# Attention feeding a Mish MLP on one core: three tiled stays per four heads instead of four, shared two-bank PSUM tiles, and Mish in half blocks

## The chip, the cores and the metric

The kernel runs on one core of one Trainium2 chip. The metric is the device time of one execution in microseconds (us), as the median of several executions. A *span* is the time from the first to the last instruction of the profiled execution; it is about 1.7 to 3 us shorter than the device time.

## The reference

Eight batches, twelve heads, 448 tokens, head size 64. The attention's softmax has an extra 1 in its denominator, its output is laid side by side over the heads, and an MLP with Mish follows.

```python
scores = scale * np.matmul(q, k.transpose(0, 1, 3, 2))        # q, k, v: (8, 12, 448, 64)
m = np.max(scores, axis=-1, keepdims=True)
e = np.exp(scores - m)
attn = e / (np.sum(e, axis=-1, keepdims=True) + np.exp(-m) + 1e-09)
x = np.matmul(attn, v)                                         # then heads side by side: (3584, 768)
h = x @ w_in                                                   # w_in: (768, 2048)
g = h * np.tanh(softplus(h))                                   # Mish
out = g @ w_out                                                # w_out: (2048, 768)
```

Multiplying numerator and denominator by exp(m) gives exp(s) / (1 + sum exp(s)), which is what the kernel computes.

## The kernel before

The program goes through the batches in passes. In pass p, TensorE does the attention of batch p between the first MLP product of batch p-1 (the `h` units, six matmuls of 448 columns) and the second one of batch p-2 (the `o` units, eight matmuls of 384 columns). A *group* is four heads, that is two pairs of heads; a pass has three groups, and groups are numbered from 0 over all batches.

Three kinds of matmul use TensorE in different shapes ("tiling modes"): the `h` and `o` units fill the array (128 x 128). The scores put two heads into two row halves (64 x 128). The sums and the product with v put four heads into four column strips (128 x 32). An uninterrupted run of tiled matmuls between full-size work is called a *stay* here.

```python
s_pool = ...tile_pool(name="s_ps", bufs=2, space=PSUM)     # score tiles, two banks each
x_pool = ...tile_pool(name="x_ps", bufs=2, space=PSUM)     # av tiles, one bank each
m_pool = ...tile_pool(name="m_ps", bufs=2, space=PSUM)     # everything else, one bank each

def sums(g):                                   # denominators of four heads
    den = m_pool.tile([128, 512], FP32, tag="m", name="den_ps")
    side_by_side(den, g, lambda c, t: ones[0:P, :])                     # 16 tiled matmuls
    rc = work.tile([128, S], FP32, tag="rc", name="rc")
    nc.scalar.activation(out=rc, in_=den[:, 0:S], func=AF.Ln, bias=1.0)
    nc.scalar.activation(out=rc, in_=rc, func=AF.Exp, scale=-1.0)       # rc = 1 / (1 + den)
    rc_t[g] = rc

def attend(g, s):                              # half s of the head size
    ...
    av = x_pool.tile([128, 512], FP32, tag="x", name="av_ps")           # a tile for each half
    side_by_side(av, g, lambda c, t: ...v_t[g]...[:, c, t, s])          # 16 tiled matmuls
    nc.vector.tensor_mul(x_t[b][:, gi, s, :], av[:, 0:S], rc_t[g])

def mish(b):                                   # the whole batch at once, on ScalarE
    ...
    nc.scalar.activation(out=gt[:, :, o : o + TAIL], in_=h_sb[:, :, MAIN:S], func=AF.Mish)
    for i in range(4):
        ...
        nc.scalar.activation(out=gm[:, f, :], in_=h_sb[:, f, 0:MAIN], func=AF.Mish)
    nc.scalar.preload_act_table_set("natural_log_exp_and_others")

def slot(j, units, pre=0, mish_of=None):       # one pair of heads; j even also does a group's av
    ...
    run(units, pre)
    g = j // 2 - 1 if j % 2 == 0 and j >= 2 else None
    if g is not None:
        sums(g)
    ...
    scores(j, (0, 1))                          # four matmuls, two exps on ScalarE
    if g is not None:
        attend(g, 0)
        attend(g, 1)
    run(units, (len(units) + 1) // 2)
    ...
    scores(j, (2, 3))
    run(units)
```

`side_by_side` issues 16 matmuls into four column strips; `scores(j, tiles)` issues two matmuls for each score tile and one exp that reads it. A score tile's buffer is free again when its exp has read it.

The softmax here doesn't subtract the row's maximum and nothing guards it: scores larger than these inputs give would overflow.

## Time and profile before

| | |
|---|---|
| device time, median | 459.04 us (3 runs, 457.97 to 459.19) |
| span | 456.1 us |
| TensorE busy | 435.1 us, 95% |
| a pass from 150 us on, mean of four | 51.45 us |
| granted TensorE clock, mean | 0.98 |

Three lines of the page of the profile: the busy time of each engine, the granted TensorE clock in tenths over 40 slices of the span, and the engines of the chain of work that ended last.

```profile
PE 435.1 (95%) x3424; PEld 211.2 (46%) x3424; DVE 139.5 (31%) x232; ACT 265.1 (58%) x323; POOL 87.9 (19%) x144
...
PEclk9898999799989999999999999999999999999999
...
PE 84%; ACT 7%; DMA 6%; POOL 1%; issue 1%; DVE 0%; POOLq 0%
```

TensorE (PE) is the bound. Only a change of its own instruction stream, or of what it waits for, can move the time.

The timeline of PE over one group of a later pass follows: start and length in us, line, output and inputs, number of matmuls. The difference of two starts is what a block costs, because consecutive matmuls overlap at their ends.

```profile
201.61 0.94 PE L177 MATMUL den_ps<-e,ones 112*32 112x448 bf16 x16
202.48 0.59 PE L154 MATMUL s_ps<-qk 64*112 64x448 bf16 x4
202.99 1.70 PE L177 MATMUL av_ps<-e,v_b 112*32 112x448 bf16 x32
204.62 2.44 PE L211 MATMUL h_ps<-xT,w_in_sb 128*128 128x448 bf16 x12
207.00 0.59 PE L154 MATMUL s_ps<-qk 64*112 64x448 bf16 x4
207.52 2.44 PE L211 MATMUL h_ps<-xT,w_in_sb 128*128 128x448 bf16 x12
...
215.67 0.94 PE L177 MATMUL den_ps<-e,ones 112*32 112x448 bf16 x16
```

Nothing waits here: no line carries a bracket with idle time. The stay den, scores, av takes 3.01 us (201.61 to 204.62), and three stays of four score matmuls follow in the group.

What waits there are stand early in the run. These lines of the list of waits give the total in us, how often, and the longest.

```profile
PE s_ps L154 <- ACT e L161: 7.9, 7, 4.4
...
PE tr_ps L137 <- DMA kq<-in_k_dram: 2.9, 2, 2.2
```

The 7.9 us are mostly the first two Mish blocks, which keep ScalarE away from the exps that free the score tiles.

### The profile page before, as it was taken

What the parts mean: (1) busy time and instruction counts of PE and PEld (TensorE: products, weight loads), DVE (VectorE), ACT (ScalarE), POOL (GpSimd) and SP (SyncE); (2) the same over time, 40 slices, a digit from 0 to 9 for tenths busy, and PEclk for the clock granted to TensorE, in tenths of its full rate; (3) what the DMA queues carried; (4) which work ended last, traced back from release to release, by engine and by line L of the source; (5) the groups of instructions that cost most, each with busy time, mean ns of one, the idle gap of its engine ahead of it and who ended that gap; (6) DMA issues with size and microseconds to landing.
All of it is one profiled execution on the core that took longest, in us unless ns stands there. A gap on an engine that the chain in (4) does not pass through costs nothing.

```text
span 456.1 us, 8023 instructions
## 1 busy us (share of the span) xinstructions
PE 435.1 (95%) x3424; PEld 211.2 (46%) x3424; DVE 139.5 (31%) x232; ACT 265.1 (58%) x323; POOL 87.9 (19%) x144
## 2 busy tenths in 40 slices
PE   8789998599979999999999999999999999999995
PEld 3334443244534446444554446444554445555563
DVE  2223543133203442244313442234313442210121
ACT  5586559754865558564865558564775559442200
POOL 6444214011111420142011410143011100000000
PEclk9898999799989999999999999999999999999999
DMA  9999999241357911893156911794056401210122
GB/s 203 202 204 204 189 165 220 62 101 44 84 132 163 225 59 36 166 295 94 30 140 163 239 55 34 182 273 101 22 144 163 95 1 34 71 36 27 44 69 69
DMA packets 77540, 55.21 MB, mean 121 GB/s; under 512 B 36544, under 2 KB 73920, under 8 KB 77504
## 3 DMA queue, kind: packets, MB, share of 16 engines
q1 hardware_dynamic: 64288, 44.51, 41.2%
q0 software_dynamic: 13216, 10.19, 14.5%
q8 instruction: 26, 0.43, 0.4%
q14 instruction: 10, 0.08, 0.1%
HBM read 45.61 MB, written 11.01 MB: 124 GB/s over the span
## 4 chain that ended last, share of the span: by engine, by line
PE 84%; ACT 7%; DMA 6%; POOL 1%; issue 1%; DVE 0%; POOLq 0%
PE h_ps L211 31%; PE o_ps L263 31%; PE s_ps L154 9%; PE av_ps L177 8%; PE den_ps L177 4%; ACT e L161 3%; DMA kq<-in_q_dram 3%; DMA w_in_sb<-in_moe_w_in_dram 3%; ACT gm L240 2%; POOL kq L100 1%; PE tr_ps L137 1%; ACT L241 1%; ACT L237 1%; ACT gt L237 0%; POOL w_in_sb L293 0%
## 5 line engine op out<-in xcount | busy, mean ns | idle before, releaser
L161 ACT ACTIVATE e<-s_ps 112x896 bf16<-112x896 f32 x192 | 164.5, 912 | 103.5 <-PE s_ps L154 103.3
L211 PE MATMUL h_ps<-xT,w_in_sb 128*128 128x448 bf16 x768 | 159.5, 356 | 1.1 <-DVE h_sb L219 1.1
L263 PE MATMUL o_ps<-w_out_sb,gm 128*128 128x384 bf16 x768 | 132.1, 328 | 0.0
L211 PEld LDWEIGHTS <-w_in_sb 128*128 128x128 bf16 x768 | 70.6, 98 | 81.1 <-issue 23.5
L263 PEld LDWEIGHTS <-gm 128*128 128x128 bf16 x768 | 74.1, 98 | 55.3 <-issue 7.8
L219 DVE COPY h_sb<-h_ps 128x448 f32<-128x448 f32 x112 | 69.9, 624 | 96.6 <-PE h_ps L211 94.4
L271 DVE COPY o_sb<-o_ps 128x384 f32<-128x384 f32 x56 | 31.2, 558 | 140.7 <-PE o_ps L263 135.4
L154 PE MATMUL s_ps<-qk 64*112 64x448 bf16 x384 | 61.3, 382 | 8.9 <-ACT e L161 7.9
L116 POOL CAST kq<-k_f 112x512 bf16<-112x512 f32 x36 | 22.1, 614 | 192.6 <-DMA k_f<-in_k_dram 173.0
L203 DVE TENSOR_TENSOR xT<-av_ps,rc 128x448 bf16<-128x448 f32 x48 | 29.9, 625 | 48.9 <-PE av_ps L177 46.0
L177 PE MATMUL av_ps<-e,v_b 112*32 112x448 bf16 x768 | 41.2, 357 | 0.0
L154 PEld LDWEIGHTS <-qk 64*112 64x112 bf16 x384 | 19.6, 126 | 46.2 <-issue 42.3
L240 ACT ACTIVATE gm<-h_sb 128x1536 bf16<-128x1536 f32 x28 | 39.1, 1467 | 0.0
L189 ACT ACTIVATE rc<-den_ps 128x448 f32<-128x448 f32 x24 | 13.1, 546 | 39.2 <-PE den_ps L177 39.2
L120 POOL CAST v_b<-v_f 112x512 bf16<-112x512 f32 x36 | 22.1, 613 | 49.5 <-PE av_ps L177 38.6
L177 PEld LDWEIGHTS <-v_b 112*32 112x32 bf16 x768 | 18.6, 97 | 19.9 <-issue 6.7
L177 PE MATMUL den_ps<-e,ones 112*32 112x448 bf16 x384 | 23.6, 367 | 0.0
L116 POOL CAST kq<-q_f 112x512 bf16<-112x512 f32 x36 | 22.1, 614 | 5.2 <-DMA q_f<-in_q_dram 4.1
L263 PE MATMUL o_ps<-w_out_sb,gt 128*128 128x384 bf16 x128 | 22.5, 326 | 0.0
L223 ACT ACTIVATE gm<-h_ps 128x384 bf16<-128x384 f32 x16 | 7.8, 490 | 21.2 <-PE h_ps L211 21.2
L263 PEld LDWEIGHTS <-gt 128*128 128x128 bf16 x128 | 12.0, 98 | 9.5 <-issue 2.0
L177 PEld LDWEIGHTS <-ones 112*32 112x32 bf16 x384 | 8.4, 97 | 12.9 <-issue 9.3
(27 smaller groups left out, 102.9 us busy)
## 6 DMA issues: line engine op xcount, KB each, us to landing
k_f<-in_k_dram SPq DMA_DIRECT2D x37, 224.0 KB, 3.6
q_f<-in_q_dram SPq DMA_DIRECT2D x37, 224.0 KB, 3.8
v_f<-in_v_dram SPq DMA_DIRECT2D x36, 224.0 KB, 4.0
w_in_sb<-in_moe_w_in_dram POOLq DMA_DIRECT2D x8, 384.0 KB, 12.6
w_out_sb<-in_moe_w_out_dram POOLq DMA_DIRECT2D x4, 768.0 KB, 17.4
out_dram<-o_sb SPq DMA_DIRECT2D x8, 336.0 KB, 2.9
out_dram<-o_sb SPq DMA_DIRECT2D x8, 288.0 KB, 2.7
out_dram<-o_sb SPq DMA_DIRECT2D x8, 240.0 KB, 2.7
```

Source lines behind the costliest of these rows:

```text
L116: nc.gpsimd.tensor_copy(out=mb[:, i].rearrange("p t h d -> p h t d"), in_=loaded.pop((j, name)).rearrange("p h (t d) -> p h t d", d=D),)
L120: nc.gpsimd.tensor_copy(out=vb[:, o : o + 2], in_=loaded.pop((j, "v")))
L154: nc.tensor.matmul(sp[0:P, h, 0:S], lhsT=qk[r, 0, t * P : (t + 1) * P], rhs=qk[r, 1, :], start=True, stop=True,)
L161: nc.scalar.activation(out=e_t[j][:, t], in_=sp[0:P, :, 0:S], func=AF.Exp, scale=SCALE)
L177: nc.tensor.matmul(ps[c * 32 : c * 32 + 32, 0:S], lhsT=weights(c, t), rhs=e_t[2 * g + c // 2][:, t, c % 2, :], start=(t == 0), stop=(t == ...
L189: nc.scalar.activation(out=rc, in_=den[:, 0:S], func=AF.Ln, bias=1.0)
L203: nc.vector.tensor_mul(x_t[b][:, gi, s, :], av[:, 0:S], rc_t[g])
L211: nc.tensor.matmul(hp[:, 0:S], lhsT=w_in_sb[:, dm // 2, dm % 2, ff * 128 : (ff + 1) * 128], rhs=x_t[b][:, dm // 2, dm % 2, :], start=(dm = ...
L219: nc.vector.tensor_copy(out=h_sb[:, ff, :], in_=hp[:, 0:S])
L240: nc.scalar.activation(out=gm[:, f, :], in_=h_sb[:, f, 0:MAIN], func=AF.Mish)
L263: nc.tensor.matmul(op[:, 0:HALF], lhsT=lhs, rhs=w_out_sb[:, ff, n * HALF : (n + 1) * HALF], start=(ff == 0), stop=(ff == FF_T - 1),)
L271: nc.vector.tensor_copy(out=o_sb[:, n * HALF : (n + 1) * HALF], in_=op[:, 0:HALF])
```

## The change

The intent: fewer changes of the tiling mode on TensorE, fewer gaps around Mish, earlier arrival of k and q at the start, a shorter tail. Two pairs of heads become one `group_slot` with three stays: den, av and two score tiles; three score tiles; three score tiles. For three score tiles in one stay, three two-bank PSUM tiles are needed. The separate av tiles had to go, so av takes one of the three, with its two halves in its two banks. Mish runs in two halves, one in each of two groups (`gates_of` says which half a `group_slot` runs).

```diff
-    s_pool = ctx.enter_context(tc.tile_pool(name="s_ps", bufs=2, space=PSUM))
-    x_pool = ctx.enter_context(tc.tile_pool(name="x_ps", bufs=2, space=PSUM))
+    s_pool = ctx.enter_context(tc.tile_pool(name="s_ps", bufs=3, space=PSUM))
...
-    def attend(g, s):
+    def attend(g):
...
-        av = x_pool.tile([128, 512], FP32, tag="x", name="av_ps")
-        side_by_side(av, g, ...)
-        nc.vector.tensor_mul(x_t[b][:, gi, s, :], av[:, 0:S], rc_t[g])
+        av = s_pool.tile([128, 2, 512], FP32, tag="s", name="av_ps")
...
+        for s in range(2):
+            side_by_side(av[:, s], g, lambda c, t: vs[:, c, t, s])
+            nc.vector.tensor_mul(x_t[b][:, gi, s, :], av[:, s, 0:S], rc)
...
-    def mish(b):
+    def mish(b, i):                  # half i: 8 of the 16 blocks of h
...
+    def group_slot(u, after_a, after_b, after_c, gates_of=None):
+        prepare(2 * u)
+        sums(u - 1)
+        if gates_of is not None:
+            mish(*gates_of)
+        attend(u - 1)
+        if 2 * u < J:
+            scores(2 * u, (0, 1))
+        run(after_a)
...
+        scores(2 * u, (2, 3))
+        scores(2 * u + 1, (0,))
+        run(after_b)
...
+        scores(2 * u + 1, (1, 2, 3))
+        run(after_c)
...
+            else:                    # passes 3 to 7
+                n = len(m2)
+                group_slot(u, cut(m2, n // 2 - 4), cut(m1, 4), cut(m1, 4))
+                group_slot(u + 1, cut(m1, 5), m1, cut(m2, 2), (p - 1, 0))
+                group_slot(u + 2, cut(m2, 4), cut(m2, n // 4 - 1 & ~1), m2, (p - 1, 1))
```

Cut: the order of the loads (k and q of groups 2 and 3 go ahead of most of w_in), the units of passes 1 and 2, and the tail, where the last eviction is split over VectorE and ScalarE and its two stores go out from two queues.

More of the change, by code (lines that the diff above doesn't have):

```diff
@@ L191, in sums @@
         rc_t[g] = rc
-    def attend(g, s):
+    def attend(g):
         b, gi = divmod(g, GRP)
-        if gi == 0 and s == 0:
+        if gi == 0:
             x_t[b] = work.tile([128, GRP, 2, S], BF16, tag="xT", name="xT")
-        av = x_pool.tile([128, 512], FP32, tag="x", name="av_ps")
-        side_by_side(
-            av,
-            g,
-            lambda c, t: v_t[g].rearrange("p c (t d s) -> p c t s d", s=2, d=D // 2)[:, c, t, s],
-        )
-        nc.vector.tensor_mul(x_t[b][:, gi, s, :], av[:, 0:S], rc_t[g])
-        if s == 1:
-            e_t.pop(2 * g), e_t.pop(2 * g + 1), v_t.pop(g)
-            rc_t.pop(g)
+        av = s_pool.tile([128, 2, 512], FP32, tag="s", name="av_ps")
+        vs = v_t.pop(g).rearrange("p c (t d s) -> p c t s d", s=2, d=D // 2)
+        rc = rc_t.pop(g)
+        for s in range(2):
+            side_by_side(av[:, s], g, lambda c, t: vs[:, c, t, s])
+            nc.vector.tensor_mul(x_t[b][:, gi, s, :], av[:, s, 0:S], rc)
+        e_t.pop(2 * g), e_t.pop(2 * g + 1)
     def mm1(b, ff, direct):
@@ L236, in mish @@
         n = FF_T // 4
-        nc.scalar.activation(out=gt[:, :, o : o + TAIL], in_=h_sb[:, :, MAIN:S], func=AF.Mish)
-        for i in range(4):
-            f = slice(i * n, (i + 1) * n)
+        f = slice(2 * i * n, (2 * i + 2) * n)
+        nc.scalar.activation(out=gt[:, f, o : o + TAIL], in_=h_sb[:, f, MAIN:S], func=AF.Mish)
+        for f0 in (2 * i * n, (2 * i + 1) * n):
+            f = slice(f0, f0 + n)
             nc.scalar.activation(out=gm[:, f, :], in_=h_sb[:, f, 0:MAIN], func=AF.Mish)
@@ L270, in mm2 @@
         if part == 1:
-            nc.vector.tensor_copy(out=o_sb[:, n * HALF : (n + 1) * HALF], in_=op[:, 0:HALF])
+            cols = slice(n * HALF, (n + 1) * HALF)
+            if b == B - 1 and t == NC:
+                q0, q1 = n * HALF, n * HALF + HALF // 2
+                nc.vector.tensor_copy(out=o_sb[:, q0:q1], in_=op[:, 0 : HALF // 2])
+                nc.scalar.copy(o_sb[:, q1 : q1 + HALF // 2], op[:, HALF // 2 : HALF])
+                for i, eng in enumerate((nc.sync, nc.scalar)):
+                    rows = out[(b - 1 + i) * S : (b + i) * S, cols]
+                    rows = rows.rearrange("(p t) n -> t p n", t=NT)[NT - 1, P - TAIL : P]
+                    eng.dma_start(out=rows, in_=o_sb[i * TAIL : (i + 1) * TAIL, cols])
+                return
+            nc.vector.tensor_copy(out=o_sb[:, cols], in_=op[:, 0:HALF])
             if n == 1:
@@ L303, in load_w_out @@
         )
-    fetch = {
-        2: [lambda: load_cast(3, "kq"), lambda: load_w_in(3)],
-        3: [lambda: load_cast(3, "v"), lambda: load_w_out(0)],
-        4: [lambda: load_cast(4, "kq")],
-        5: [lambda: load_cast(4, "v"), lambda: load_w_out(1)],
-        6: [lambda: load_cast(5, "kq")],
-        7: [lambda: load_cast(5, "v"), lambda: load_w_out(2), lambda: load_w_out(3)],
-    }
     def first_slot(j):
-        for f in fetch.get(j, ()):
-            f()
         g = j // 2 - 1 if j % 2 == 0 and j >= 2 else None
+        if j % 2:
+            g3 = 3 + j // 2
+            load_cast(g3, "kq")
+            if j == 1:
+                load_cast(2, "v")
+            else:
+                load_cast(g3 - 1, "v")
+            load_w_in(1 + j // 2)
         scores(j, (0,))
@@ L330, in first_slot @@
         if g is not None:
-            attend(g, 0)
-            attend(g, 1)
+            attend(g)
         scores(j, (3,))
@@ L339, in run, with prepare @@
             units.pop(0)()
-    def slot(j, units, pre=0, mish_of=None):
-        for f in fetch.get(j, ()):
-            f()
+    def prepare(j):
         if SW <= j + 2 < J:
@@ L349, in slot @@
             load(j + 4)
-        run(units, pre)
-        g = j // 2 - 1 if j % 2 == 0 and j >= 2 else None
-        if g is not None:
-            sums(g)
-        if mish_of is not None:
-            mish(mish_of)
-        if j < J:
-            scores(j, (0, 1))
-        if g is not None:
-            attend(g, 0)
-            attend(g, 1)
-        run(units, (len(units) + 1) // 2)
-        if j + 1 < J:
-            transposes(j + 1)
-        if j < J:
-            scores(j, (2, 3))
-        run(units)
+    def group_slot(u, after_a, after_b, after_c, gates_of=None):
[7 more added lines that the diff above has]
+        run(after_a)
+        if 2 * u >= J:
+            return
+        if u == GRP:
+            transposes(2 * u + 1)
+        transposes(2 * u + 2)
+        prepare(2 * u + 1)
+        scores(2 * u, (2, 3))
+        scores(2 * u + 1, (0,))
+        run(after_b)
+        transposes(2 * u + 3)
+        scores(2 * u + 1, (1, 2, 3))
+        run(after_c)
     def cut(m, n):
@@ L379 @@
         load_cast(1, "kq")
+        load_cast(2, "kq")
         load_w_in(0)
         load_cast(1, "v")
-        load_cast(2, "kqv")
-        load_w_in(1)
-        load_w_in(2)
         idle(8)
@@ L388 @@
         transposes(0)
-        for p in range(B):
-            m1 = mm1_units(p - 1) if p >= 1 else []
+        for j in range(NPAIR):
+            first_slot(j)
+        for p in range(1, B):
+            m1 = mm1_units(p - 1)
             m2 = mm2_units(p - 2) if p >= 2 else []
-            for i in range(NPAIR):
-                j = p * NPAIR + i
-                if p == 0:
-                    first_slot(j)
-                elif p == 1:
-                    slot(j, cut(m1, (2, 3, 3, 3, 3, 2)[i]))
-                elif p == 2:
-                    if i == 0:
-                        slot(j, cut(m1, 6), mish_of=0)
-                    elif i in (1, 3):
-                        slot(j, cut(m1, 1) + cut(m2, 2) + cut(m1, 1), pre=1)
-                    elif i < 5:
-                        slot(j, cut(m1, 4), pre=1)
-                    else:
-                        slot(j, m2, pre=1)
-                elif i == 0:
-                    slot(j, cut(m2, len(m2) - 10 + p % 2 * -2), pre=1)
-                elif i < 5:
-                    slot(j, cut(m1, 4), pre=1)
-                else:
-                    slot(j, m2, pre=1)
-                if i == 4 and p >= 2:
-                    mish(p - 1)
-                    run(cut(m2, len(m2) * 2 // 3))
+            u = p * GRP
+            if p == 1:
+                load_w_out(0)
+                group_slot(u, cut(m1, 1), cut(m1, 2), cut(m1, 2))
+                load_cast(5, "v")
+                load_w_out(1)
+                load_w_out(2)
+                load_w_out(3)
+                group_slot(u + 1, cut(m1, 2), cut(m1, 2), cut(m1, 2))
+                group_slot(u + 2, cut(m1, 2), cut(m1, 2), m1, (0, 0))
+            elif p == 2:
+                group_slot(u, cut(m1, 4), cut(m1, 4), cut(m1, 4), (0, 1))
+                group_slot(u + 1, m1, cut(m2, 2), cut(m2, 2), (1, 0))
+                group_slot(u + 2, cut(m2, 4), cut(m2, 2), m2, (1, 1))
+            else:
+                n = len(m2)
+                group_slot(u, cut(m2, n // 2 - 4), cut(m1, 4), cut(m1, 4))
+                group_slot(u + 1, cut(m1, 5), m1, cut(m2, 2), (p - 1, 0))
+                group_slot(u + 2, cut(m2, 4), cut(m2, n // 4 - 1 & ~1), m2, (p - 1, 1))
         m2 = mm2_units(B - 2)
-        slot(J, cut(m2, 4), pre=2)
+        run(cut(m2, 2))
+        group_slot(B * GRP, cut(m2, 2), [], [])
         m1 = mm1_units(B - 1, direct=True)
```

## The prediction

> **What bounds it.** TensorE. The page's first part has it busy 435.1 of 456.1 us (95%); the chain of waits runs 84% on it. In the timeline from 135 us on it never idles until the last store; a pass (one batch) takes 51.45 us. The first pass waits for DMA (2.9 us at 11 to 15 us, 1.55 us at 32 to 34 us) and ends at 39.7 us. Around the first two Mish blocks it waits for ScalarE (5.7 us near 80, 2.3 us near 129). Each long gap drops the granted clock to 0.5 (windows table): about 1.5 us more.
>
> **What a mode change costs (timeline, start to start).** Two matmuls of a score tile add 0.19 us; four in a stay take 0.515 us, so leaving costs 0.135. Two h units take 2.38 us before a tiled stay, 2.27 among full-size work: 0.11. den takes 0.87 before scores, 0.77 directly before av (396.5 us): 0.10. The Trainium skill, "TensorEngine Tiling (Array Packing)", Key Properties, says a mode change drains the array; this trace agrees, at 0.10 to 0.135 us.
>
> **Removed.** Per four heads ten changes become seven: the stay den, scores, av becomes den, av, scores, and one full/scores/full detour goes. About 0.35 us; 21 groups give 7.4 us, all critical.
>
> **Added.** Mish in halves: 14 halves instead of 7 blocks. A half costs 1.29 (table load) + 0.53 + 2.86 + 1.29 (load back) = 6.0 us of ScalarE against 9.2 for a whole block, affordable on average (265 busy of 456). But the half stands before the exps of the first two score tiles, and with three score buffers the fourth score tile needs the first exp. From the start of den: rc ready 2.06, half Mish done 8.04, first exp frees its buffer at about 9.0, second at 9.8. TensorE reaches the fourth tile at about 8.9 with five h units between (steady passes, first half) and 8.4 with four o units (second half). So about 0.7 and 1.2 us of new waiting for ScalarE: 1.9 us per steady pass against 1.06 saved, +4 us over five passes. In passes 1 and 2 a similar sum replaces the old gaps: the first half has only two h units as cover (about 4 us and slow clock), the next three wait 1.2 to 1.9 each. Only the mode changes are gained: -2 us.
>
> **Moved.** k and q of group 3 are fetched ahead of three quarters of w_in, so the wait at 32 to 34 us and the slow clock after it should go: -3.5 us. The wait at 11 to 15 us stays: its loads keep their place. Tail: the last eviction and its stores are split over two engines: -0.7 us.
>
> **Sum.** -3.5 - 2 + 4 - 0.7 = about -2; I say 456.0 us, 8 in 10 within 449 to 462. Faster by over 2%: 0.14; within 2%: 0.80; slower: 0.06.
>
> **Signs.** Right: about 63 fewer mode changes; den followed by av at 0.77; the list of waits shows scores waiting on exp about 14 times, mostly 0.5 to 1.3 us; 14 pairs of table loads; no DMA wait at 32 us, first h unit by 36 to 37 us; steady pass near 52 us. Wrong: a steady pass near 50.4 us without waits (total then near 446 us), or clock drops after the new waits (+1.5 us each, total above 461).
>
> **What would make it wrong.** Waits that lower the clock; w_in late for the first h units; late casts on GpSimd.

## The result, and the profile after

| | before | after |
|---|---|---|
| device time, median | 459.12 us (4 runs, 457.97 to 460.43) | 469.99 us (4 runs, 469.33 to 471.21) |
| span | 456.1 us | 467.7 us |
| TensorE busy | 435.1 us, 95% | 427.6 us, 91% |
| a pass from 150 us on | 51.45 us | 54.27 us |

The ratio is 1.0239 (95% interval 1.0202 to 1.0276), slower. Ratios here and below are the mean time of one kernel's fast runs over that of the kernel before in the same rounds, so they are not quite the ratio of the medians quoted. All four runs of the kernel before lie within 0.6% of each other.

TensorE is busy for 7.5 us less, yet the span grows by 11.6 us. (In the four passes from den of group 9 on, where the granted clock is 1.00 in both profiles, the busy time falls from 51.43 to 50.80 us a pass, as fewer mode changes promise. The rest of the 7.5 us lies where the clock or the amount of work differs too.) Where it grows can be read from the starts of den. The first `h` unit starts at 39.71 us before and 39.72 after. den of group 9 starts at 150.02 and 151.04. Then four passes take 4 x 51.45 and 4 x 54.27 us, which is 11.3 us more. So the loss is in the steady passes, where the prediction had seen +0.8 us a pass and +2.8 is measured.

The work up to group 9 is not the same. From the first `h` unit to den of group 9 the kernel before issues 222 matmuls of `h` and the changed kernel 240. These 18 take about 3.5 us (an estimate from 30 of them in 5.78 us, 209.55 to 215.33 below), and the changed kernel has them less at its end. For equal work, then, passes 1 and 2 became about 2.5 us shorter. The stretch from den of group 21 to the last matmul takes 95.18 and 95.08 us, so about 3.4 us more for equal work.

The same lines of the page after, without the clock:

```profile
PE 427.6 (91%) x3424; PEld 215.8 (46%) x3424; DVE 139.4 (30%) x232; ACT 285.3 (61%) x346; POOL 87.0 (19%) x144
...
PE 78%; ACT 13%; DVE 3%; DMA 3%; issue 1%; POOL 1%; DVEq 0%; POOLq 0%
```

ScalarE and VectorE are now in the chain that ended last. The PE timeline of one group, in a slot with a half Mish:

```profile
205.31 0.94 PE L176 MATMUL den_ps<-e,ones 112*32 112x448 bf16 x16
206.07 0.93 PE L176 MATMUL av_ps<-e,v_b 112*32 112x448 bf16 x16
208.16 0.94 PE L176 MATMUL av_ps<-e,v_b 112*32 112x448 bf16 x16 [1.16 <-DVE xT L201]
209.03 0.59 PE L153 MATMUL s_ps<-qk 64*112 64x448 bf16 x4
209.55 5.85 PE L207 MATMUL h_ps<-xT,w_in_sb 128*128 128x448 bf16 x30
215.33 0.77 PE L153 MATMUL s_ps<-qk 64*112 64x448 bf16 x6
216.04 3.58 PE L207 MATMUL h_ps<-xT,w_in_sb 128*128 128x448 bf16 x18
...
222.96 0.94 PE L176 MATMUL den_ps<-e,ones 112*32 112x448 bf16 x16
```

The 32 matmuls of av are broken in two. Between the halves TensorE is idle for 1.16 us, released by VectorE's multiply into xT. The list of waits shows that this is no single case:

```profile
PE av_ps L176 <- DVE xT L201: 27.4, 24, 1.2
...
PE s_ps L153 <- ACT e L160: 3.3, 4, 2.1
```

It happens in each of the 24 groups. The timeline of all engines inside the gap shows what the multiply waits for:

```profile
206.30 0.54 ACT L188 ACTIVATE rc<-den_ps 128x448 f32<-128x448 f32 x1 [3.37 <-PE den_ps L176]
206.88 0.58 ACT L189 ACTIVATE rc<-rc 128x448 f32<-128x448 f32 x1
...
207.48 0.62 DVE L201 TENSOR_TENSOR xT<-av_ps,rc 128x448 bf16<-128x448 f32 x1 [1.45 <-ACT rc L189]
208.16 0.94 PE L176 MATMUL av_ps<-e,v_b 112*32 112x448 bf16 x16 [1.16 <-DVE xT L201]
```

The chain den, Ln, Exp, multiply stands in full between the two halves of av. The second half writes the other bank of the tile, which the multiply does not read.

Also to be seen: the expected waits of the scores on exp are nearly absent (3.3 us, none in a steady pass).

### The profile page after: what moved, and what is told of

Read it like the earlier page. It is cut to its first block, busy times and chain, and to the rows that moved or that the text cites. A ratio compares the mean times of both kernels' runs of the same rounds, so it can differ in the third digit from the quotient of the medians.

```text
span 467.7 us, 8046 instructions
## 1 busy us (share of the span) xinstructions
PE 427.6 (91%) x3424; PEld 215.8 (46%) x3424; DVE 139.4 (30%) x232; ACT 285.3 (61%) x346; POOL 87.0 (19%) x144
## 4 chain that ended last, share of the span: by engine, by line
PE 78%; ACT 13%; DVE 3%; DMA 3%; issue 1%; POOL 1%; DVEq 0%; POOLq 0%
PE o_ps L261 31%; PE h_ps L207 29%; PE s_ps L153 8%; PE av_ps L176 4%; PE den_ps L176 4%; ACT e L160 4%; ACT rc L189 3%; DVE xT L201 3%; ACT rc L188 3%; DMA kq<-in_q_dram 3%; ACT gm L238 2%; ACT L239 1%; ACT L235 1%; PE tr_ps L136 1%; DMA out_dram<-o_sb 0%
## 5 line engine op out<-in xcount | busy, mean ns | idle before, releaser
L160 ACT ACTIVATE e<-s_ps 112x896 bf16<-112x896 f32 x192 | 162.7, 917 | 82.7 <-PE s_ps L153 81.9
L207 PE MATMUL h_ps<-xT,w_in_sb 128*128 128x448 bf16 x768 | 152.5, 353 | 0.0
L207 PEld LDWEIGHTS <-w_in_sb 128*128 128x128 bf16 x768 | 72.4, 98 | 74.5 <-issue 10.9
L261 PEld LDWEIGHTS <-gm 128*128 128x128 bf16 x768 | 72.9, 98 | 55.1 <-issue 8.6
L279 DVE COPY o_sb<-o_ps 128x384 f32<-128x384 f32 x54 | 30.1, 558 | 150.1 <-PE o_ps L261 136.7
L176 PE MATMUL av_ps<-e,v_b 112*32 112x448 bf16 x768 | 45.3, 353 | 27.4 <-DVE xT L201 27.4
L153 PE MATMUL s_ps<-qk 64*112 64x448 bf16 x384 | 55.5, 373 | 4.0 <-ACT e L160 3.3
L176 PEld LDWEIGHTS <-v_b 112*32 112x32 bf16 x768 | 20.9, 96 | 46.7 <-issue 34.1
L153 PEld LDWEIGHTS <-qk 64*112 64x112 bf16 x384 | 20.8, 126 | 36.1 <-issue 29.1
L261 PE MATMUL o_ps<-w_out_sb,gt 128*128 128x384 bf16 x128 | 21.5, 326 | 0.0
L239 ACT ACT_TABLE_LOAD x14 | 18.0, 1283 | 0.3
L235 ACT ACT_TABLE_LOAD x14 | 18.0, 1283 | 0.2
```

Of the source, the lines that this page charges most:

```text
L153: nc.tensor.matmul(sp[0:P, h, 0:S], lhsT=qk[r, 0, t * P : (t + 1) * P], rhs=qk[r, 1, :], start=True, stop=True,)
L160: nc.scalar.activation(out=e_t[j][:, t], in_=sp[0:P, :, 0:S], func=AF.Exp, scale=SCALE)
L176: nc.tensor.matmul(ps[c * 32 : c * 32 + 32, 0:S], lhsT=weights(c, t), rhs=e_t[2 * g + c // 2][:, t, c % 2, :], start=(t == 0), stop=(t == ...
L207: nc.tensor.matmul(hp[:, 0:S], lhsT=w_in_sb[:, dm // 2, dm % 2, ff * 128 : (ff + 1) * 128], rhs=x_t[b][:, dm // 2, dm % 2, :], start=(dm = ...
L235: nc.scalar.activation(out=gt[:, f, o : o + TAIL], in_=h_sb[:, f, MAIN:S], func=AF.Mish)
L261: nc.tensor.matmul(op[:, 0:HALF], lhsT=lhs, rhs=w_out_sb[:, ff, n * HALF : (n + 1) * HALF], start=(ff == 0), stop=(ff == FF_T - 1),)
```

## The experiments

All results were correct against the reference.

**Both halves of av, then both multiplies.** The theory: the second half waits because both halves are one PSUM tile and the multiply that reads the tile stands between them in the program.

```diff
         for s in range(2):
             side_by_side(av[:, s], g, lambda c, t: vs[:, c, t, s])
+        for s in range(2):
             nc.vector.tensor_mul(x_t[b][:, gi, s, :], av[:, s, 0:S], rc)
```

> Both av halves are multiplied on TensorE before VectorE scales either. Theory (the wait comes from both halves being one PSUM tile: the second half's first matmul waits until VectorE has read the first half, which waits for rc): the 24 waits of av on xT (27.4 us in the changed kernel) go, den to the end of av takes 0.77+1.63 us, but the waits of scores on exp behind the half Mish, which the 1.16 us delay was hiding, come back: about 0.7 and 1.2 us in the two halves of a steady pass. Total 454 us (451 to 458). Rival (the chain den, Ln, Exp, multiply bounds the slot anyway, so TensorE only waits elsewhere): 467 to 471 us.

Measured: 457.05 us (454.40 to 459.65), before 458.13, ratio 0.9987 (0.9946 to 1.0027): the same as the kernel before. The PE timeline of two groups with a half Mish, in one steady pass:

```profile
202.84 0.94 PE L176 MATMUL den_ps<-e,ones 112*32 112x448 bf16 x16
203.61 1.69 PE L176 MATMUL av_ps<-e,v_b 112*32 112x448 bf16 x32
205.23 0.58 PE L153 MATMUL s_ps<-qk 64*112 64x448 bf16 x4
205.75 5.85 PE L208 MATMUL h_ps<-xT,w_in_sb 128*128 128x448 bf16 x30
211.53 0.83 PE L153 MATMUL s_ps<-qk 64*112 64x448 bf16 x4
212.76 0.40 PE L153 MATMUL s_ps<-qk 64*112 64x448 bf16 x2 [0.41 <-ACT e L160]
213.09 3.58 PE L208 MATMUL h_ps<-xT,w_in_sb 128*128 128x448 bf16 x18
...
228.22 0.40 PE L153 MATMUL s_ps<-qk 64*112 64x448 bf16 x2
229.13 0.40 PE L153 MATMUL s_ps<-qk 64*112 64x448 bf16 x2 [0.51 <-ACT e L160]
229.93 0.40 PE L153 MATMUL s_ps<-qk 64*112 64x448 bf16 x2 [0.41 <-ACT e L160]
230.26 2.77 PE L262 MATMUL o_ps<-w_out_sb,gm 128*128 128x384 bf16 x16
```

The 32 matmuls of av are whole again. From den to the scores it takes 2.39 us; after the change it was 3.72. So a group pays 1.33 us for the split: 1.16 of waiting and 0.17 by which the broken block itself takes longer. In exchange the waits on ScalarE that the prediction had placed appear: the middle stays take 1.56 and 2.04 us, where 0.71 is normal (215.33 to 216.04 after the change), which is 0.85 and 1.33 us. The prediction had said 0.7 and 1.2. A steady pass takes 52.45 us; the prediction had said near 52. Three splits of 1.33 minus these 2.18 us are 1.81 us, and the two kernels' passes differ by 54.27 - 52.45 = 1.82 us. The delay at av had been hiding the waits on ScalarE.

**Two tiles, same order.** The order of the changed kernel stays: half, multiply, half, multiply. Only the tile differs.

```diff
-        av = s_pool.tile([128, 2, 512], FP32, tag="s", name="av_ps")
...
         for s in range(2):
-            side_by_side(av[:, s], g, lambda c, t: vs[:, c, t, s])
-            nc.vector.tensor_mul(x_t[b][:, gi, s, :], av[:, s, 0:S], rc)
+            av = s_pool.tile([128, 2, 512], FP32, tag="s", name="av_ps")
+            side_by_side(av[:, 0], g, lambda c, t: vs[:, c, t, s])
+            nc.vector.tensor_mul(x_t[b][:, gi, s, :], av[:, 0, 0:S], rc)
```

> The program order of the changed kernel is kept (half, multiply, half, multiply), but each half has a tile of its own out of the same three. Theory (the tile is what is waited for): the waits of av on xT go although the order is the same; 453 to 459 us, with a small new wait of the second score tile for the first multiply. Rival (the order alone, or rc itself, makes TensorE wait): about 470 us with 24 waits of 1.16 us.

Measured: 458.41 us (457.67 to 459.19), ratio 1.0016 (0.9977 to 1.0056). The PE timeline at the start of a group:

```profile
200.65 0.94 PE L176 MATMUL den_ps<-e,ones 112*32 112x448 bf16 x16
201.41 1.69 PE L176 MATMUL av_ps<-e,v_b 112*32 112x448 bf16 x32
203.03 0.87 PE L153 MATMUL s_ps<-qk 64*112 64x448 bf16 x4
```

VectorE's timeline at the same place:

```profile
202.82 1.16 DVE L201 TENSOR_TENSOR xT<-av_ps,rc 128x448 bf16<-128x448 f32 x2 [1.45 <-ACT rc L189]
```

av is whole although a multiply stands between its halves in the program and still waits for rc. So neither the order alone nor rc makes TensorE wait. The wait needs both a shared tile and a read of it between its two halves: this run takes away the first, both_halves_first the second, and either is enough. (The score stay after it takes 0.80 us instead of 0.52, since now its second tile waits for a buffer of av; that was expected.)

**The cost put into the kernel before.** Its two av halves get one two-bank tile, nothing else changes.

```diff
-x_pool = ctx.enter_context(tc.tile_pool(name="x_ps", bufs=2, space=PSUM))
+x_pool = ctx.enter_context(tc.tile_pool(name="x_ps", bufs=1, space=PSUM))
...
-        av = x_pool.tile([128, 512], FP32, tag="x", name="av_ps")
+        if s == 0:
+            av_t[g] = x_pool.tile([128, 2, 512], FP32, tag="x", name="av_ps")
+        av = av_t[g]
...                                   # half s is av[:, s]
```

> The kernel before, with its two av halves in one two-bank tile and nothing else changed. Theory: the cost appears here too, smaller, as scores stand between den and av: the second half starts after rc (2.06 us after den's start) and one multiply (0.62), so about 0.7 to 0.8 us per four heads, 24 times: 474 to 478 us. Rival (the wait needs the new order or the shared score buffers): 458 to 460 us.

Measured: 478.81 us (475.64 to 479.81), ratio 1.0449 (1.0406 to 1.0492), 20.7 us above the kernel before and 0.8 above the range that was expected. The list of waits, and one wait in the PE timeline of a steady group:

```profile
PE av_ps L178 <- DVE xT L206: 19.6, 24, 1.2
...
213.64 0.94 PE L178 MATMUL av_ps<-e,v_b 112*32 112x448 bf16 x16 [0.80 <-DVE xT L206]
```

The one tile alone makes the kernel before lose more than the whole change lost. In a steady group the wait is 0.80 us, shorter than 1.16, because the scores stand between den and av there and part of rc's chain has run by then.

**Mish behind the first two exps.** With the av wait gone, the position of Mish on ScalarE is the next suspect.

```diff
         sums(u - 1)
-        if gates_of is not None:
-            mish(*gates_of)
         attend(u - 1)
         if 2 * u < J:
             scores(2 * u, (0, 1))
+        if gates_of is not None:
+            mish(*gates_of)
```

> As both_halves_first, and the half Mish stands on ScalarE behind the exps of the first two score tiles. Theory (Mish ahead of those exps holds the score buffers): the waits of scores on exp shrink to below 1 us per steady pass (left: about 0.4 and 0.6 us in the second half's last stay); 446 us (443 to 450). Rival (ScalarE's total work in these slots is the limit, wherever Mish stands): as both_halves_first, 452 to 458.

> A repeat, as the partner of the next two on one chip: 446 to 449 us.

Measured: 447.84 us (ratio 0.9785, 0.9750 to 0.9821), and later 449.38 us (0.9803, 0.9780 to 0.9827), 0.4 us above the range expected for the repeat. It is faster than the kernel before in both, but whether by 2% is unclear. The list of waits of the first, where both_halves_first has 14.6 us in 23 waits:

```profile
PE s_ps L153 <- ACT e L160: 9.3, 18, 3.1
```

A steady pass takes 51.38 us, 1.07 less than in both_halves_first. The position matters, not the sum of ScalarE's work, which is the same in both kernels. Two score buffers are free before Mish begins instead of after it.

**Whole Mish blocks in the new slots.** Are halves worth seven more pairs of table loads? The edit in short (the calls for the first halves go too):

```diff
-        f = slice(2 * i * n, (2 * i + 2) * n)
+        f = slice(0, 4 * n)                       # the whole block, where the second half stood
```

> As mish_after, but each Mish is one whole block again (7 instead of 14, 18 us less ScalarE work), standing where the second half stood. Theory (halves are worth their extra table loads, because a whole block of 9.2 us outlasts the TensorE work that the three score buffers leave): 2.5 to 3 us of waiting per steady pass, some 5 us in pass 2, total 458 to 468 us. Rival (fewer table loads win): 442 to 446 us.

Measured: 475.79 us (475.36 to 477.41), ratio 1.0392 (1.0347 to 1.0438). The direction is as expected, the size is not: the estimate ended at 468. The PE timeline shows what it left out.

```profile
234.06 0.40 PE L153 MATMUL s_ps<-qk 64*112 64x448 bf16 x2 [3.00 <-ACT e L160]
234.87 0.62 PE L153 MATMUL s_ps<-qk 64*112 64x448 bf16 x2 [0.41 <-ACT e L160]
235.68 0.62 PE L153 MATMUL s_ps<-qk 64*112 64x448 bf16 x2 [0.18 <-ACT e L160]
236.23 3.74 PE L262 MATMUL o_ps<-w_out_sb,gm 128*128 128x384 bf16 x16
239.90 0.94 PE L176 MATMUL den_ps<-e,ones 112*32 112x448 bf16 x16
```

The waits in this stay add up to 3.6 us, more than the 2.5 to 3 expected, and the granted clock falls from 1.00 to 0.50 behind the first of them (at about 234.8 us): the two `o` units that follow take 3.67 us (236.23 to 239.90) instead of 2.70. Every steady pass pays that again. It takes 56.31 us, 4.9 more than in mish_after, and the run's mean granted clock is 0.96. Outside the steady passes one `h` unit also waits 3.7 us for VectorE's copies. The sum was not worked out further.

**Scores between den and av again.** One mode change more per group, to measure its price.

```diff
         sums(u - 1)
-        attend(u - 1)
         if 2 * u < J:
             scores(2 * u, (0, 1))
+        attend(u - 1)
         if gates_of is not None:
             mish(*gates_of)
```

> As mish_after, but the first two score tiles stand between den and av again, so each of the 21 groups has one more mode change (eight instead of seven) and nothing else on TensorE. Theory (a mode change costs 0.10 to 0.135 us, all on the critical path): 2 to 3 us slower than mish_after, den to scores takes 0.87 instead of 0.77; about 450 us if mish_after gives 447.8. Rival (the gain of the group slots comes from waits that went, not from mode changes): within 0.5 us of mish_after.

> A repeat whose profile should fall in the fast state. New theory for its surprise (2.5 us faster than mish_after though it has 21 mode changes more): the first two exps follow rc without the 0.68 us of idle ScalarE that mish_after has there, so each half Mish ends that much earlier and the waits of scores on exp (9.3 us in mish_after) fall to about 4 us, which outweighs the mode changes; den to scores takes 0.87. 444 to 447 us. Rival (the mode changes cost nothing on the critical path): the waits are as in mish_after, 9 us, and den, scores and av together take no longer.

Measured: 445.29 us, ratio 0.9706 (0.9672 to 0.9740), which is faster than mish_after, not slower: a miss for both theories as they were put. The profiled run (618.72 us at a mean granted clock of 0.655) is used for nothing here. The repeat gave 443.62 us, ratio 0.9684 (0.9659 to 0.9709), beside mish_after at 449.38 (0.4 us under the expected range), and a profile. Its list of waits:

```profile
PE s_ps L153 <- ACT e L160: 3.2, 4, 2.2
```

9.5 us in 18 waits (mish_after_again) became 3.2 us in 4. In mish_after ScalarE idled 0.68 us between rc and the first exp, as the scores came only after av; with the scores in front the exps follow rc at once and Mish ends earlier. The extra mode changes are there too, but they are paid back: a steady pass takes 50.82 us, against 51.38.

**Units moved to cover Mish.** From mish_after:

```diff
-                group_slot(u, cut(m1, 1), cut(m1, 2), cut(m1, 2))
+                group_slot(u, cut(m1, 1), cut(m1, 2), cut(m1, 1))
...
-                group_slot(u + 1, cut(m1, 2), cut(m1, 2), cut(m1, 2))
-                group_slot(u + 2, cut(m1, 2), cut(m1, 2), m1, (0, 0))
+                group_slot(u + 1, cut(m1, 1), cut(m1, 2), cut(m1, 1))
+                group_slot(u + 2, cut(m1, 2), cut(m1, 4), m1, (0, 0))
...
-                group_slot(u + 2, cut(m2, 4), cut(m2, n // 4 - 1 & ~1), m2, (p - 1, 1))
+                group_slot(u + 2, cut(m2, 4), cut(m2, n // 2 - 4), m2, (p - 1, 1))
```

> As mish_after with units moved so that TensorE has work while a half Mish runs: pass 1 leaves eight h units for its last group (2, 4, 2), and passes with 16 o units give the second half's middle stay four units. The wait of 3.1 us in pass 1 with its slow clock should fall below 1 us and three passes lose 0.7 us of waiting each: 3 to 5 us under mish_after, about 443 us. If the slow clock or ScalarE's backlog is the limit instead: 446 to 448 us.

Measured: 442.84 us (441.26 to 443.89), ratio 0.9660 (0.9627 to 0.9692). The longest wait on exp fell from 3.1 to 0.8 us.

**Both together, which also isolates a mode change.**

> tuned with the first two score tiles between den and av: one mode change more per group, where few waits are left to gain from. In the passes of tuned without any wait (50.24 us from den to den) the theory expects 0.3 to 0.4 us more (three changes of 0.10 to 0.135 us); in passes with a wait about as much is won back. Total within 2 us of tuned (442.8), 441.5 to 445. If mode changes cost nothing: 50.24 us again, total 439 to 441.5.

Measured: 440.39 us (438.64 to 441.97), ratio 0.9615 (0.9589 to 0.9642), under the range of the first theory, and in that of the rival (mode changes cost nothing). The totals cannot decide, because the waits differ too: those on exp are 5.1 us in 12 places in tuned and 1.2 us in 3 in tuned_between. The price of a mode change is read from a pass in which neither kernel waits. First tuned, then tuned_between, from den to the den of the same group one pass later:

```profile
243.09 0.94 PE L176 MATMUL den_ps<-e,ones 112*32 112x448 bf16 x16
243.85 1.69 PE L176 MATMUL av_ps<-e,v_b 112*32 112x448 bf16 x32
...
293.33 0.94 PE L176 MATMUL den_ps<-e,ones 112*32 112x448 bf16 x16
```

```profile
239.83 0.94 PE L176 MATMUL den_ps<-e,ones 112*32 112x448 bf16 x16
240.70 0.58 PE L153 MATMUL s_ps<-qk 64*112 64x448 bf16 x4
...
290.42 0.94 PE L176 MATMUL den_ps<-e,ones 112*32 112x448 bf16 x16
```

50.24 and 50.59 us: three more changes cost 0.35 us, 0.117 each, which is the theory's figure and not the rival's. This version is the fastest of all and beats both kernels.

**The new order of loads in the kernel before.** The order of the loads in the prologue and in the first slots is taken over, nothing else.

The edit in short, with some lines put into words:

```diff
-    fetch = {2: [k, q of group 3; w_in(3)], 3: [v of group 3; w_out(0)], ...}
+    # in slots 1, 3, 5: k, q of groups 3, 4, 5; v of groups 2, 3, 4; w_in(1), w_in(2), w_in(3)
...
         load_cast(1, "kq")
+        load_cast(2, "kq")
         load_w_in(0)
         load_cast(1, "v")
-        load_cast(2, "kqv")
-        load_w_in(1)
-        load_w_in(2)
```

> The kernel before with the new order of loads alone. Theory of the prediction: the DMA wait ahead of the transposes at 32 to 34 us (1.55 us) and the slow clock after it go, first h unit at 36 to 37 us instead of 39.7; 455 us, ratio 0.992. Rival (DMA arrival at the start differs from run to run by as much, and the first pass is bounded by ScalarE): ratio 0.997 to 1.003.

Measured: 456.79 us (455.30 to 459.26), ratio 0.9973 (0.9935 to 1.0011), between the two theories and not clear of zero. In its profile the waits at 32 to 34 us are gone and the first `h` unit starts at 37.88 us instead of 39.71. What this is worth in the median stays open: the first pass also differs between profiles of kernels that share this order (first `h` unit at 34.45 us in mish_after, 36.87 in tuned, 38.48 in both_halves_first).

## Why the prediction was wrong

The prediction was 456.0 us, within 449 to 462; measured were 469.99 us. Point by point:

- **The step that failed** is the one under "Removed": "the stay den, scores, av becomes den, av, scores", costed by mode changes alone. It took the two halves of av as one block that nothing interrupts. In the changed kernel both halves are one PSUM tile with a multiply between them, so the second half waits for rc and for the multiply: 1.33 us per group, 24 groups, about 32 us gross. Net it is about 13 us, because the same delay hides waits on ScalarE. Two_tiles shows that it is the tile, both_halves_first that it costs 2.5% net (ratio 1.0239 against 0.9987), and before_one_av_tile that it costs even more, 4.5%, in the old order. The prediction had seen that av now comes from the shared tiles, and asked when its buffer comes free for the scores, but not what a half-written tile does to its own second half.
- **Mode changes**: predicted 0.35 us per group. A pass without waits takes 50.24 us in tuned and 51.45 before, which is 0.40 us per group. (The passes before alternate between 51.32 and 51.59 us. The longer ones hold one stay of four score matmuls that takes 0.78 us instead of 0.51, so the saving lies between 0.36 and 0.45.) One change alone measures 0.117 us, or 0.35 for three. Right.
- **New waits on ScalarE**: predicted 0.7 and 1.2 us in the two halves. In the changed kernel there were none in the steady passes, because each half Mish overlaps with the av wait. With that wait removed they are 0.85 and 1.33 us. The mechanism was right, but the wait at av hid it.
- **Steady passes**: predicted +0.8 us each, measured +2.82. That is 3 x 1.33 for the split, minus 1.2 for the mode changes. Without the split, in both_halves_first, they are +1.0 us each. **Passes 1 and 2**: predicted -2 us; from the first `h` unit to den of group 9 the changed kernel takes 1.0 us more, but with 18 more matmuls of `h`, so about -2.5 for equal work; both_halves_first comes to -1.9 in the same way. Right. (In these two passes the split costs nothing net: without it TensorE waits 7.9 us on exp instead of 3.3, and the granted clock over them is 0.97 instead of 1.00.)
- **First pass**: predicted -3.5 us. The waits at 32 to 34 us went, but three av waits (0.81, 1.15 and 1.14 us) and a later arrival of the first q stood in their place, and the first `h` unit started at the same time. Alone in the kernel before, the new order gave a ratio of 0.9973, not clear of noise, so 3.5 us was too much.
- **Tail**: predicted -0.7 us. From the modelled end of the last matmul to the end of the span it is 5.1 us before and 4.5 after: -0.6. Right.

The sum without the missed wait would have been right: both_halves_first, which differs from the changed kernel only in the order that removes that wait, takes 457.05 us. This is not luck alone. In its profile, against that of the kernel before, the first pass is 1.2 us shorter (3.5 predicted), passes 1 and 2 are 1.9 shorter for equal work (2), the four steady passes are 4.0 longer and the rest up to the last matmul about 1.5 (4 predicted for all of it), and the tail is 0.6 shorter (0.7). Only the first pass is far off. (That profile is of its slowest run, 459.65 us.)

The Trainium skill, "PSUM — Partial Sum Buffer", section "PSUM bank collisions raise a hardware error", says that two engines collide in the same bank and quadrant and run clean on different banks. The trace before agrees: VectorE multiplies the first av half from 204.06 us on while TensorE is still writing the second (202.99 to 204.62).

```profile
204.06 1.31 DVE L203 TENSOR_TENSOR xT<-av_ps,rc 128x448 bf16<-128x448 f32 x2 [1.72 <-PE av_ps L177]
```

So the wait of 1.16 us was not asked for by PSUM; it comes with the tile that the program declares. How exactly the tile leads to the wait (which instruction carries the semaphore, and why) was not looked into; that it is the tile is shown.

## What to carry to other kernels

When buffers are merged to save PSUM, look at every tile that is written in parts while another engine reads an earlier part: a wait on the whole tile can put that engine's full input chain between the parts, although the banks differ. Issue all writes of a tile before its first read, or keep a tile per part. And when a wait goes, look for the one that it was hiding: here the order of work on ScalarE (the exps that free buffers before the long block that frees none) was worth about 2% (ratio 0.9987 to 0.9785), and moving the covering work after that another 1.3% (0.9785 to 0.9660).

## What the Trainium skill lacked or had wrong

- "TensorEngine Tiling (Array Packing)", Key Properties, says that a change of the tiling mode drains the array, but gives no price. Here it is 0.10 to 0.135 us by single places of the timeline, and 0.117 us by two kernels that differ by three changes in a pass (50.59 against 50.24 us).
- "ScalarE: Activation LUTs", What ACT_TABLE_LOAD costs, gives about 1283 ns for the load and about 1380 ns more for a drain, 2.66 us in all. The load is 1283 ns here too, but no drain shows beside it: in the changed kernel rc ends at 207.46 us, the load starts at 207.47, and the first Mish starts at 208.76, so a switch costs 1.29 us.
- "TensorE: Matmul & The Clock Gate", Part 1, has the clock fall to one half after an idle window of about 3.4 us. In the kernel before it fell to 0.5 at 130.8 us, after an idle stretch of 1.89 us and a second one of 0.41 with two matmuls between; in mish_whole it fell at about 234.8 us, after 3.00 us and a second one of 0.41. But in the changed kernel stretches of 2.10 and 0.41 us, also with two matmuls between (70 to 73 us), left it at 1.00. So in these traces the length of the gap alone does not decide.
- No page that was read says that short waits inside a tiled stay can cost more than the idle time that the profile lists: with waits of 0.31 and 0.41 us (0.72 together, counted from modelled ends of matmuls) a stay of tuned takes 1.84 us instead of 0.71, so 1.13 us more.
- No page that was read covers one execution of a single-core program that ran at a granted clock of 0.655 from the second fortieth of its span to the end (616.9 us of span); its cause stays open.
